# Two attention-and-mixer layers on one core: repacked score banks, an earlier buffer release, fillers in any dead bank, and an instruction order searched from a plan

## The chip, the cores and the metric

The kernel runs on one core of one Trainium2 chip. The metric is the device time of one execution in microseconds (us).

Five engines share the work: PE (TensorE, matmuls; its weight loads are listed as PEld), ACT (ScalarE), DVE (VectorE), POOL (GpSimd) and SP (SyncE, which issues DMA). A profile is one execution. "L955" is line 955 of that kernel, so the same instruction has another line number in each kernel.

## The reference

Two identical layers, each a layer norm, 16-head attention with a residual add, a layer norm and a mixer block with an MLP. S = 2048 tokens, D = 448, head size 28, F = 1792, bf16 inputs.

```python
def _A_ref(x, wqkv, wo):                 # attention, H = 16, Dh = 28
    q, k, v = ...                        # x @ wqkv, split into heads
    p = softmax(einsum("bhqd,bhkd->bhqk", q, k) * Dh ** -0.5)
    return merge_heads(einsum("bhqk,bhkd->bhqd", p, v)) @ wo

def _B_ref(x, w1, w2, w3, w4):           # mixer and MLP
    h = gelu(layernorm(x) @ w1)
    hs = concat(h's four quarters, shifted by +1, -1, +2, -2 tokens) @ w2
    x1 = x + hs
    return x1 + gelu(layernorm(x1) @ w3) @ w4

x = A_x                                  # the next two lines, twice
x = x + _A_ref(layernorm(x), A_wqkv, A_wo)
x = x + _B_ref(layernorm(x), B_w1, B_w2, B_w3, B_w4)
```

(The names are shortened here; the softmax is over the keys and the GELU is the tanh form.)

## The kernel before

A Python scheduler in the kernel's own file emits it. Every piece of work is a generator, a *task* with a priority. The scheduler has a model of how long each instruction takes and when its inputs are ready. It plays the kernel through in that model and so fixes one static order of instructions for each engine; the chip then runs these orders, with semaphores where engines depend on one another. What the model calls the end of the kernel is its *estimate*.

The 2048 tokens are 16 tiles of 128. A *unit* is a group of query tiles whose attention runs together: four units of four tiles in layer 0; in layer 1 three of four tiles (units 0 to 2) and two *half units* of two tiles (units 3 and 4). Scores go to five PSUM banks of 512 columns, in groups of three banks and two in turn; each group is one exponential on ACT. During attention a sixth bank takes the sums of P times V, and banks 6 and 7 serve everything else.

Score matmuls, with the two shapes. A half unit has only 256 queries, so it fills the 512 columns of a bank with two heads: one 64-row matmul over two heads' keys, against queries in which the other head's rows have been made zero.

```python
# q_proj, for a half unit: two copies of the queries, each with the other head's rows masked
if nw == 256:
    for h in (1, 0):
        yield op("dve", c_b2b(nw), lambda e, h=h: e.tensor_scalar(
            out=qT[:, g, q0 + 256*h : q0 + 256*h + 256], in0=qT[:, g, q0:q0 + 256],
            scalar1=cols[:, 2 + h:3 + h], scalar2=None, op0=ALU.mult), ...)
...
# st_ops: the scores of one group
for k, (si, i, j) in enumerate(grans[n]):
    ...
    bk = gbank(n) + k
    kc = kcol(L, kts[i])
    r0, rn = (32 * j, 32) if nt == 4 else (64 * j, 64)
    yield op("pe", ..., lambda e, ...: e.matmul(
        out=ps[:, bk, :], lhsT=kT[r0:r0 + rn, g, kc:kc + 128],
        rhs=qT[r0:r0 + rn, g, q0:q0 + 512], start=True, stop=True, tile_position=(r0, 0)), ...)
```

The mixer keeps its activations hT of eight tiles (HR = 8) in a ring. `t_mixA` (layer norm and w1) of a tile waits until the tile whose slot it takes, and that tile's neighbours, are finished. "Finished" means here: the whole MLP is done.

```python
def t_mixA(L, tiles, direct):
    for t in tiles:
        for tp in (t - HR - 1, t - HR, t - HR + 1):
            if 0 <= tp < NT:
                yield ("wait", ("mixBt", L, tp))
    ...                                    # statistics, normalise, transpose, w1, GELU into hT

def t_x1(L, t, i, xs):                     # spawned by t_mixB
    ...                                    # four w2 matmuls: the last readers of hT
    ...                                    # residual add, statistics, normalise

def t_mixB(L, tiles, direct, prio):
    ...                                    # t_x1 of each tile, w3, GELU, then per tile w4 and the residual add
        yield ("sig", ("x2", L, t))
        yield ("sig", ("mixBt", L, t))     # frees the slot in hT
```

Where its model sees PE idle, the scheduler puts in *fillers*, matmuls whose result nobody reads, put there to keep PE's clock up. They may use two of the eight banks:

```python
SC.fill = (0.13, lambda e, b: e.matmul(out=ps[:, bi(b), 0:256], lhsT=ident[:, :], rhs=wv[:, 0, 0:256], ...),
           ["b6", "b7"], ...)
...
for t in self.tasks: ...                   # a candidate of each task that is ready
    ...                                    # on PE and DVE a task of lower priority is held back where
                                           # it would delay one of higher priority
    key = (ready if eng == "act" else start, t[0], t[1])       # t[0] is the fixed priority
```

Some PSUM evacuations can go to DVE or ACT (`alt=[alt("act", ...)]`); the scheduler takes the engine that would end sooner. The softmax exponentials are always on ACT, and w3's results are copied by DVE and then given to ACT in one GELU over all 14 blocks (128x7168 for four tiles); only in the last unit does ACT take each block straight from PSUM.

## Time and profile before

| | before |
|---|---|
| median (lowest to highest) of 4 runs | 1169.1 us (1163.9 to 1169.3) |
| span of the profiled run | 1167.1 us |
| ACT busy, ACT idle | 1047.7, 119.4 us |
| last exponential ends; rest to the end ("tail") | 1080.9; 86.2 us |
| scheduler's own estimate | 1164.6 us |

The prediction below shows the lines of the page and of the timeline. Two further lines help to read it. The first is from the page of the kernel before: the chain that ended last, followed back from the end, as shares of the span.

```profile
ACT 44%; PE 39%; DVE 14%; DMA 1%; issue 1%; POOL 0%; SPq 0%; DVEq 0%
```

ACT is the busiest engine on the way to the end, but 39% and 14% are PE and DVE: the stretches where ACT waits. The second view gives busy time by stretch for the kernel before. Its columns are the stretch, its length, the busy time of PE, PEld, DVE, ACT and POOL with instruction counts, PE's granted clock (1.00 is full), the DMA share and GB/s. The stretches are the layer boundary, the middle of layer 1 and the tail.

```profile
525.20:556.00 30.80, 26.38 (x156) 13.06 (x155) 15.21 (x36) 14.52 (x9) 1.02 (x1) 0.97 0.14 33
787.80:875.30 87.50, 81.56 (x498) 26.63 (x498) 53.55 (x135) 71.94 (x65) 4.03 (x5) 0.80 0.09 23
1080.90:1167.10 86.20, 78.82 (x623) 50.55 (x617) 50.33 (x130) 27.90 (x61) 5.99 (x11) 1.00 0.11 30
```

Length minus ACT's busy time is ACT's idle time, which the prediction adds up; these three stretches hold 90 of the 119 us. From 796 to 808 PE is busy for 3.14, 2.70 and 2.86 of each 4 us, and the clock is 1.00; from 808 to 812 it is 0.73 and from 812 to 824 0.50.

### The profile page before, as it was taken

Reading aid. Unit: us, or ns where it says so; the run is one execution under the profiler, and the core shown is the slowest. Engines: PE = TensorE matmul, PEld = TensorE weight load, DVE = VectorE, ACT = ScalarE, POOL = GpSimd, SP = SyncE. Lnnn points to the kernel's source line nnn. Section 1 sums busy time; section 2 is a strip of 40 time slices with the busy share of each in tenths; the row PEclk is TensorE's granted clock in tenths of the full one; section 3 lists DMA queues with packets and bytes.
Section 4 is the critical chain, followed back from the end, with each engine's and each line's share of the span. In section 5 each row is a group of like instructions: output and inputs, shape, how many; then the busy total and the mean of one; then the engine's idle time right before and its main releaser. Section 6 shows DMA issues by size and latency. Waiting matters only on the chain.

```text
span 1167.1 us, 18576 instructions
## 1 busy us (share of the span) xinstructions
PE 1091.1 (93%) x7799; PEld 406.0 (35%) x7799; DVE 649.7 (56%) x1566; ACT 1047.7 (90%) x955; POOL 58.4 (5%) x76
## 2 busy tenths in 40 slices
PE   4899999989999999998999999998999999899998
PEld 1222333333332323334233323332333333333565
DVE  7876356523573255734767462557542574447952
ACT  5799999999999999994999999998889999999144
POOL 4000000000010000000001000000000010001000
PEclk9999999999999999999999999998779999999999
DMA  7122160000000000000111112321000110010011
GB/s 170 37 82 64 32 157 19 15 1 19 19 18 2 19 19 19 12 8 19 28 37 42 28 46 63 83 55 45 10 15 1 31 28 1 1 31 14 23 31 35
DMA packets 79213, 40.18 MB, mean 34 GB/s; under 512 B 63960, under 2 KB 72536, under 8 KB 79128
## 3 DMA queue, kind: packets, MB, share of 16 engines
q1 hardware_dynamic: 77544, 36.23, 12.2%
q0 software_dynamic: 1584, 2.75, 0.8%
q8 instruction: 61, 1.00, 0.3%
q14 instruction: 24, 0.20, 0.1%
HBM read 13.75 MB, written 8.13 MB: 19 GB/s over the span
## 4 chain that ended last, share of the span: by engine, by line
ACT 44%; PE 39%; DVE 14%; DMA 1%; issue 1%; POOL 0%; SPq 0%; DVEq 0%
ACT PT L955 38%; PE ps L932 9%; PE ps L979 7%; PE ps L1259 5%; PE ps L1239 4%; PE ps L1302 4%; ACT h2T L1254 4%; PE ps L695 3%; PE ps L756 2%; PE ps L1118 2%; DVE x1b L1194 1%; PE ps L715 1%; PE ps L1050 1%; DVE x_res L1197 1%; DVE st L1199 1%
## 5 line engine op out<-in xcount | busy, mean ns | idle before, releaser
L955 ACT ACTIVATE PT<-ps 128x1536 bf16<-128x1536 f32 (+1 forms) x821 | 940.2, 1258 | 45.9 <-PE ps L932 37.7
L932 PE MATMUL ps<-qT,kT 32*128 32x512 bf16 (+1 forms) x2048 | 335.8, 392 | 13.8 <-ACT PT L955 9.1
L979 PE MATMUL ps<-PT,vaug 128*32 128x512 bf16 (+1 forms) x2304 | 232.5, 368 | 3.1 <-ACT PT L955 1.8
L1302 PE MATMUL ps<-wv,ident 128*128 128x256 bf16 x1102 | 168.2, 279 | 8.8 <-DVE kT L704 2.2
L932 PEld LDWEIGHTS ps<-qT,kT 32*128 32x128 bf16 (+1 forms) x2048 | 79.4, 91 | 253.7 <-ACT PT L955 176.2
L1248 DVE CAST h2T<-ps 128x512 bf16<-128x512 f32 (+2 forms) x126 | 73.9, 586 | 113.0 <-PE ps L1239 112.2
L1239 PE MATMUL ps<-xT,w 128*128 128x512 bf16 (+3 forms) x672 | 129.0, 311 | 0.3
L1302 PEld LDWEIGHTS ps<-wv,ident 128*128 128x128 bf16 x1102 | 93.5, 99 | 82.3 <-issue 45.7
L1259 PE MATMUL ps<-w,h2T 128*128 128x448 bf16 x448 | 101.0, 358 | 11.4 <-ACT h2T L1254 11.4
L979 PEld LDWEIGHTS ps<-PT,vaug 128*32 128x32 bf16 x2304 | 57.2, 94 | 125.8 <-issue 88.6
L1262 DVE TENSOR_TENSOR x_res<-x_res,ps 128x448 f32<-128x448 f32 x32 | 19.8, 618 | 120.5 <-PE ps L1259 120.5
L1239 PEld LDWEIGHTS ps<-xT,w 128*128 128x128 bf16 x672 | 49.6, 97 | 58.4 <-issue 32.3
L1254 ACT ACTIVATE h2T<-h2T 128x7168 bf16<-128x7168 bf16 (+2 forms) x9 | 45.1, 5015 | 20.2 <-DVE h2T L1248 20.1
L1259 PEld LDWEIGHTS ps<-w,h2T 128*128 128x128 bf16 x448 | 38.7, 98 | 60.1 <-issue 19.5
L994 DVE COPY u_sb<-ps 128x512 f32<-128x512 f32 (+1 forms) x36 | 22.7, 629 | 37.1 <-PE ps L979 36.1
L1118 PE MATMUL ps<-xT,w 128*112 128x512 bf16 (+2 forms) x160 | 40.8, 364 | 0.6 <-DVE x1b L1194 0.6
L695 PE MATMUL ps<-xT,wk_pad 128*128 128x512 bf16 x128 | 39.8, 398 | 1.1 <-DVE qT L739 0.8
L695 PE MATMUL ps<-xT,wq_pad 128*128 128x512 bf16 (+1 forms) x144 | 38.6, 369 | 0.8 <-DVE qT L739 0.7
L1067 DVE TENSOR_SCALAR hT<-ps 112x512 f16<-112x512 f32 (+1 forms) x32 | 21.0, 655 | 31.0 <-PE ps L1118 31.0
L998 DVE SCALAR_TENSOR_TENSOR u_sb<-uin,fct,ps 128x512 f32<-128x512 f32 x24 | 17.9, 747 | 36.1 <-PE ps L979 34.2
L1050 PE MATMUL ps<-wo_pad,otn 128*128 128x448 bf16 x128 | 35.8, 362 | 2.0 <-DVE x_res L1054 1.3
L620 DVE BATCH_NORM_STATS2 st<-x_res 128x6 f32<-128x448 f32 x60 | 37.0, 618 | 1.0
(138 smaller groups left out, 852.0 us busy)
## 6 DMA issues: line engine op xcount, KB each, us to landing
uscr<-u_sb SPq DMA_DIRECT2D x24, 256.0 KB, 2.7
uin<-uscr SPq DMA_DIRECT2D x24, 256.0 KB, 2.8
x_res<-in_A_x_dram POOLq DMA_DIRECT2D x3, 896.0 KB, 12.0
out_dram<-uin SPq DMA_DIRECT2D x16, 112.0 KB, 1.7
w<-in_B_w_dram SPq DMA_DIRECT2D x1, 1568.0 KB, 15.6
w<-in_B_w_dram SPq DMA_DIRECT2D x1, 1344.0 KB, 10.7
h2T<-in_A_wqkv_dram SPq DMA_DIRECT2D x2, 336.0 KB, 6.5
xT<-xn SPq DMA_TRANSPOSE x37, 3.6
```

The source lines that it names most:

```text
L620: yield op("dve", 0.55, lambda e: e.bn_stats(out=st6[:, t, :], in_=w4[:, t, :] if staged else x_res[:, t, :]), reads=[("w4",) if staged el ...
L695: yield op("pe", c_mm(nw), lambda e, fc=fc, rows=rows, b=b: e.matmul(out=ps[:, bi(b), 0:nw], lhsT=wpad[0:rows, fc, 128 * g:128 * g + 128], ...
L932: yield op("pe", 0.225 if k == 0 else 0.005 if nt == 4 or k == 1 else 0.215, lambda e, bk=bk, r0=r0, rn=rn, g=g, kc=kc, q0=q0: e.matmul(ou ...
L955: yield op("act", 0.077 + 0.427 * cnt, lambda e, b0=b0, p0=p0, cnt=cnt: e.activation(out=PT[:, p0:p0 + cnt, :], in_=ps[:, b0:b0 + cnt, :], ...
L979: yield op("pe", 0.055 if nt == 4 else 0.035, lambda e, j=j, rhs=rhs, vs=vs, i=i: e.matmul(out=ps[32 * j:32 * j + 32, UBK, 0:128 * nt], lh ...
L1050: yield op("pe", c_mm(D), lambda e, g=g, tt=tt, b=b: e.matmul(out=ps[:, bi(b), 0:D], lhsT=otn[:, g, 128 * tt:128 * tt + 128], rhs=wo_pad[: ...
L1118: yield op("pe", c_mm(NW), lambda e, fc=fc, rows=rows, grp=grp, b=b: e.matmul(out=ps[0:112, bi(b), 0:NW], lhsT=w1[0:rows, fc, 112 * grp:11 ...
L1239: yield op("pe", c_mm(NW), lambda e, fc=fc, rows=rows, fch=fch, b=b: e.matmul(out=ps[:, bi(b), 0:NW], lhsT=w3[0:rows, fc, 128 * fch:128 * ...
L1248: yield op("dve", c_ps(NW), lambda e, fch=fch, b=b: e.tensor_copy(out=h2T[:, fch, hoff:hoff + NW], in_=ps[:, bi(b), 0:NW]), reads=[("ps", ...
L1254: yield op("act", c_act(14 * NW), lambda e: e.activation(out=h2T[:, :, hoff:hoff + NW], in_=h2T[:, :, hoff:hoff + NW], func=ACT.Gelu_apprx ...
L1259: yield op("pe", c_mm(D), lambda e, fch=fch, i=i, b=b: e.matmul(out=ps[:, bi(b), 0:D], lhsT=h2T[:, fch, hoff + 128 * i:hoff + 128 * i + 12 ...
L1302: SC.fill = (0.13, lambda e, b: e.matmul(out=ps[:, bi(b), 0:256], lhsT=ident[:, :], rhs=wv[:, 0, 0:256], start=True, stop=True), ["b6", "b ...
```

## The change

The intent, read from the diff, is fourfold: make the half units' score matmuls as cheap as the full units'; free a slot of hT as soon as nothing reads it any more; allow a filler in any bank whose contents are dead; and replace the fixed priorities by an order that comes from a plan, improved by a search.

```diff
@@ score banks of the half units: two key tiles of one head, no masked queries @@
-            if nw == 256:
-                for h in (1, 0):
-                    yield op("dve", c_b2b(nw), lambda e, h=h: e.tensor_scalar(...))
...
-                    r0, rn = (32 * j, 32) if nt == 4 else (64 * j, 64)
-                    yield op("pe", ..., lambda e, ...: e.matmul(
-                        out=ps[:, bk, :], lhsT=kT[r0:r0 + rn, g, kc:kc + 128],
-                        rhs=qT[r0:r0 + rn, g, q0:q0 + 512], start=True, stop=True, tile_position=(r0, 0)),
+                for (h, k, si, i, j) in sorted(mms):
+                    W = 128 * nt
+                    kt = kts[4 // nt * i + h]
+                    kc = kcol(L, kt)
+                    yield op("pe", ..., lambda e, ..., c0=W * h: e.matmul(
+                        out=ps[:, bk, c0:c0 + W], lhsT=kT[r0:r0 + 32, g, kc:kc + 128],
+                        rhs=qT[r0:r0 + 32, g, q0:q0 + W], start=True, stop=True, tile_position=(r0, 0)),
@@ early release of hT @@
-                        yield ("wait", ("mixBt", L, tp))
+                        yield ("wait", ("x1", L, tp))
...                                        # in t_x1, right after the four w2 matmuls
+            yield ("sig", ("x1", L, t))
@@ fillers @@
-                if self.busy.get(b, False):
+                if key(b) in self.live:
...
-                   ["b6", "b7"], ...
+                       ["b6", "b7", "b5", "b4", "b3", "b2", "b1", "b0"], ...
@@ order @@
-                for t in sorted(self.tasks, key=lambda x: (x[0], x[1])):
+                    todo.sort(key=self.rank)          # rank: the latest start in the plan
...
-            for grp in range(4):
+            def group(grp):                            # groups of a step become tasks of their own
...
+            yield from par(3, [group(grp) for grp in range(4)])
...
+        plan = None
+        for k in range(ROUNDS):                        # ROUNDS = 2
+            res = attempt(plan)
+            plan = res[2].latest_starts(res[0])
+        for seed in SEEDS:                             # 181 numbers
+            plan = reorder(plan, seed)
+        est, P, SC = attempt(plan)
```

`latest_starts` goes backwards through one played schedule and gives each instruction the latest time at which it may start without lengthening that schedule. `reorder` adds seeded random shifts to some of these times. Cut from the diff: memoisation in the scheduler, the bookkeeping of live banks, more places where loops become `par`, and new constants of the model (for instance PELAT from 0.12 to 0.04 and a table switch from 1.35 to 1.42).

## The prediction

> **What bounds the kernel now.** I read the page first: busy shares, then the forty slices, then the costliest groups.
>
> ```profile
> PE 1091.1 (93%) x7799; PEld 406.0 (35%) x7799; DVE 649.7 (56%) x1566; ACT 1047.7 (90%) x955; POOL 58.4 (5%) x76
> ...
> ACT  5799999999999999994999999998889999999144
> ...
> PEclk9999999999999999999999999998779999999999
> ...
> L955 ACT ACTIVATE PT<-ps 128x1536 bf16<-128x1536 f32 (+1 forms) x821 | 940.2, 1258 | 45.9 <-PE ps L932 37.7
> ```
>
> PE looks busiest, but its matmuls overlap and 168 us of its 1091 are the 1102 filler matmuls (L1302), there only to keep its clock up. The softmax exponentials on ACT, 821 of them, are 940 us of a 1167 us span, and slice after slice of ACT reads 9. So ACT is the bound, and **what can be won is ACT's idle time**, 1167.1 - 1047.7 = 119.4 us. The busy time by stretch says where it lies (stretch length minus ACT busy): start 0 to 27.9: 13.9; 27.9 to 58.4: 7.3; 58.4 to 525.2: 5.3; the layer boundary 525.2 to 556: 16.3; 556 to 787.8: 1.6; 787.8 to 875.3: 15.6; 875.3 to 1080.9: 1.1; the tail after the last exponential, 1080.9 to 1167.1: 58.3. Together 119.4.
>
> The timeline names three of these holes:
>
> ```profile
> 531.69 6.18 ACT L1254 ACTIVATE h2T<-h2T 128x7168 bf16<-128x7168 bf16 x1
> ...
> 556.01 2.37 ACT L955 ACTIVATE PT<-ps 128x1024 bf16<-128x1024 f32 x2 [16.24 <-PE ps L932]
> ...
> 803.04 7.80 ACT L955 ACTIVATE PT<-ps 128x1024 bf16<-128x1024 f32 x7 [4.41 <-PE ps L979]
> ```
>
> At the boundary, layer 1's scores need the first layer's MLP, whose GELU comes only at 531.7, when the attention of layer 0 is already over. In layer 1 a late normalisation stops ACT 4.4 us at 803, PE idles with it, and its clock drops (busy times in 4 us windows; the column after the engines is the granted clock):
>
> ```profile
> 812.00:816.00 4.00, 4.00 (x23) 1.06 (x16) 2.36 (x6) 3.53 (x4) 0.00 (x0) 0.50 0.24 53
> 816.00:820.00 4.00, 4.00 (x20) 1.03 (x19) 0.94 (x4) 2.96 (x3) 0.00 (x0) 0.50 0.29 66
> 820.00:824.00 4.00, 4.00 (x19) 0.78 (x16) 2.44 (x5) 2.47 (x3) 0.00 (x0) 0.50 0.01 2
> ```
>
> PE now really is full, and ACT runs 2.5 to 3.5 of 4 us. The same comes back at 856 to 868.
>
> The tail is a backlog of MLP work. A whole four-tile MLP, that of unit 2, runs after all attention is over, and only then does the last unit's chain begin (its statistics start at 1117.5):
>
> ```profile
> 1094.80 12.26 PE L1239 MATMUL ps<-xT,w 128*128 128x512 bf16 x56
> ...
> 1107.89 6.18 ACT L1254 ACTIVATE h2T<-h2T 128x7168 bf16<-128x7168 bf16 x1 [15.56 <-DVE h2T L1248]
> ...
> 1114.12 10.77 PE L1259 MATMUL ps<-w,h2T 128*128 128x448 bf16 x56 [1.22 <-ACT h2T L1254]
> ```
>
> Why so late? Unit 2's out-projection is done at 981.3, but its mixer's statistics wait until 1031.3:
>
> ```profile
> 1030.79 0.62 DVE L1262 TENSOR_TENSOR x_res<-x_res,ps 128x448 f32<-128x448 f32 x1 [5.61 <-PE ps L1259]
> 1031.33 0.62 DVE L620 BATCH_NORM_STATS2 st<-x_res 128x6 f32<-128x448 f32 x1
> ```
>
> They start 0.54 us after the second residual add of unit 1's MLP. That is the code's wait for "mixBt", the end of the whole MLP of the tile whose slot in the eight-tile ring hT is to be reused: 50 us of waiting.
>
> [...]
>
> **The change, part by part.**
>
> *Score banks of the half units* (last two units of layer 1). Before, a 64-row matmul of 512 columns made two heads against a zero-padded query, so only two row groups could run together and a three-bank group took two passes:
>
> ```profile
> 1001.41 0.60 PE L932 MATMUL ps<-qT,kT 64*128 64x512 bf16 x3
> ...
> 1002.48 0.39 PE L932 MATMUL ps<-qT,kT 64*128 64x512 bf16 x2
> ```
>
> After, two 32-row matmuls of 256 columns fill each bank and up to four heads run together. Matmuls become 2048 - 256 + 512 = 2304; a three-bank group should take 0.39, as the full units' x3 groups do. The number of banks is unchanged (32 items per segment either way), so ACT's 821 exponentials stay. 256 banks are some 51 pairs of groups: 51 x 0.21 = **10.7 us of PE time freed**, all of it between 945 and 1081, where PE has no slack. The 16 masking copies (L746, 283 ns) take 4.5 us off DVE, beside other work. On ACT directly: nothing.
>
> *The early release of hT* (signal after the w2 matmuls instead of after w4). Unit 1's w2 matmuls finish near 950 and unit 2's out-projection at 981, so the mixer of unit 2 can start some 50 us sooner. Its w3 and w4 (12.3 + 10.8 = 23 us of PE) then have to fit before 1081. Room: the 10.7 us freed, and the fillers of 787.8 to 1080.9, 183 at about 0.12 us each = 22 us (0.12 from runs such as 17 in 2.02 us). It fits, if the order is good. The tail then is the last unit's own chain: 9.5 us from the last exponential to its last out-projection add (1080.9 to 1090.4), plus 49.6 us from its statistics to the end (1117.5 to 1167.1) = 59; less about 5 because unit 3's two-tile w4 (1138.8 to 1144.2) can move into the chain's waits: 54. Against 86.2 that is -32. But the GELU of 6.18 us and two table loads, 8.7 us, move into attention, where ACT is full: **net -23**.
>
> *Order from an iterated plan.* Fixed priorities give way to latest start times of a previous plan, groups within one step become independent tasks, and 181 seeded shuffles were evidently kept because they shortened the modelled schedule. At the boundary, layer 0's last MLP is now recognised as critical; I take 12 of the 16.3 us as won, since a chain of projection, key maximum and bias (549 to 556, 7 us) is partly exposed. In 787.8 to 875.3 I take 12 of 15.6. At the start, 4 of the 7.3 us.
>
> *Filler in any dead bank.* It adds PE work only where the plan sees PE idle, and helps keep the clock at 1.00 when banks 6 and 7 are taken. Its gain is in the 12 just counted.
>
> Sum: -23 - 12 - 12 - 4 = -51, so 1169 - 51 = **1118 us**.
>
> **Rivals.** (1) *The freed PE time changes nothing*, because ACT is the bound: then only the order counts, the four-tile MLP stays in the tail, and the time is about 1169 - 28 = 1141. For it: ACT is 99% busy from 875 to 1081. Against it: the tail is PE work waiting for PE work, and 50 us of one wait is removed by the code. (2) *The plan is fitted to its own model*: static per-engine orders from 181 shuffles leave every wait tight, and small slips on the chip (more mode switches, fillers waiting for ACT, PE overrunning in 945 to 1081) open many small ACT waits. Before, waits of ACT on scores outside the named holes are only a few us; 20 us of such waits would give 1138. (3) *PE becomes the bound in the second half*, with half-clock spells as at 812: those cost about 11 us before; if they recur twice over, 1140. (4) *Better than counted*: all holes close and the tail shrinks to 48; the floor is 27.9 start + 1005.8 ACT work in attention + 8.7 moved + 48 = 1090.
>
> **Range and chances.** The terms are largely independent and each could fail by half, so I centre on 1118, with 1097 (most of rival 4) and 1141 (rival 1 or 2) as the ends of the 8 in 10 range. Two per cent is 23.4 us, below 1145.7: it takes two of the four terms failing to miss it. Faster 0.91, same 0.08, slower 0.01.
>
> **What would show it.** L955 still at 821 and near 940 us; score matmuls 2304 with 32 rows only, three-bank groups of the half units near 0.39 us; unit 2's mixer statistics before 1000 and its 128x7168 GELU before the last exponential; the tail 50 to 60 us; the hole at the boundary under 6 us; PEclk at 9 in all slices after the middle; ACT idle near 70 us in all. Wrong would be: a four-tile w3 still after the last exponential, ACT waits on scores spread over the whole of attention, or half-clock windows with more filler.

Figures for what it says of the chip, from the profile of the kernel before:

- *PE's matmuls overlap.* The 1792 score matmuls of 32 rows take 393 ns each in the mean, 704 us if added up, but PE is busy with them for 285.0 us.
- *Heads that run together.* Of the three 64-row matmuls at 1001.41 the first two start 3 ns apart and the third 0.22 us later. Of the 32-row matmuls of the full units three start within 7 ns at 700.26, and four within 10 ns at 27.24 and 555.36.
- *Mode switches.* After a filler matmul the next matmul starts 0.11 us later if it has a tile of the same shape (median of 890), 0.21 us later if it has 32 rows (median of 159).
- *Table loads.* Each of the 15 in attention and GELU takes 1283 ns. The GELU at 1013.96 starts 1.29 us after the start of its load, at 1012.67, and no idle time stands before the load.
- *No slack from 945 to 1081.* PE is busy for 127.3 of these 136 us, at a clock of 1.00.

## More of the kernel before

The runs were made on several chips, and every round ran the kernel before as well: its medians lay between 1168.3 and 1169.1 us.

## The result

| | before | after |
|---|---|---|
| median | 1169.1 us of 4 runs | 1130.3 us of 4 runs |
| lowest to highest | 1163.9 to 1169.3 | 1128.5 to 1136.5 |
| ratio, 95% interval | | 0.9688, 0.9641 to 0.9735 |
| ACT busy, ACT idle | 1047.7, 119.4 | 1056.2, 70.6 |
| tail after the last exponential | 86.2 | 49.6 |
| scheduler's own estimate | 1164.6 | 1125.7 |

A ratio is the mean time of one kernel's runs over the mean of the other's runs of the same rounds, so it is not quite the ratio of the medians beside it. The change is **faster by 3.1%**. The prediction was 1118 us within 1097 to 1141. The profiled run of the kernel after, used in all that follows, has a span of 1126.8 us.

From the page of the kernel after: busy times, the chain by engine, ACT and PE's clock in forty slices, and the exponentials.

```profile
PE 1063.9 (94%) x8094; PEld 407.6 (36%) x8094; DVE 613.8 (54%) x1527; ACT 1056.2 (94%) x972; POOL 55.7 (5%) x76
...
ACT  5899999999999999999789999999899999999954
...
PEclk9999999999999999999989999999899999999999
...
ACT 65%; PE 29%; DVE 3%; DMA 1%; issue 1%; SPq 0%; POOL 0%; ACTq 0%; DVEq 0%
...
L1108 ACT ACTIVATE PT<-ps 128x1536 bf16<-128x1536 f32 (+1 forms) x821 | 937.9, 1254 | 23.1 <-PE ps L1082 18.3
```

The exponentials are as many and as long as before (821; 940.2 and 937.9 us). What went down is the wait in front of them, 45.9 to 23.1 us, and the idle slices at the end: they read 1, 4 and 4 before and now 5 and 4. ACT carries 65% of the chain instead of 44%. But ACT's busy time *rose* by 8.5 us, which nobody had counted on.

The busy time of the kernel after by stretch, with the same three stretches (the boundary's is longer, because its holes now come later):

```profile
525.20:585.00 59.80, 56.92 (x350) 18.69 (x348) 43.70 (x109) 47.80 (x45) 3.04 (x3) 0.94 0.13 32
787.80:875.30 87.50, 81.86 (x577) 29.25 (x576) 61.26 (x154) 82.95 (x73) 6.51 (x7) 0.94 0.11 27
1077.20:1126.80 49.60, 43.65 (x400) 29.05 (x395) 27.39 (x72) 20.28 (x57) 3.73 (x7) 0.99 0.12 33
```

ACT's idle time there is 12.0, 4.6 and 29.3 us. Taking every stretch in this way gives the whole account, here against the prediction's terms:

| stretch (us of the span) | ACT idle before | after | moved | predicted |
|---|---|---|---|---|
| 0 to 58.4 | 21.2 | 17.4 | -3.8 | -4 |
| 58.4 to 525.2 | 5.3 | 0.9 | -4.4 | 0 |
| 525.2 to 787.8, the boundary and behind it | 17.9 | 13.8 | -4.1 | -12 |
| 787.8 to 875.3 | 15.6 | 4.6 | -11.0 | -12 |
| 875.3 to the last exponential | 1.1 | 4.7 | +3.6 | 0 |
| after the last exponential | 58.3 | 29.3 | -29.0 | -23 net |
| **ACT idle** | **119.4** | **70.6** | **-48.8** | **-51** |
| **ACT busy** | 1047.7 | 1056.2 | +8.5 | 0 |
| **span** | 1167.1 | 1126.8 | -40.3 | -51 |

Read the tail's row with care: the prediction's -23 is the tail's whole shortening (-32) less 8.7 us of ACT work that moves into attention. Measured in the same way, the tail is 36.6 us shorter, less 7.6 us of ACT work that left it.

The ACT timeline of the kernel after (start, length, what, in brackets the idle time before it and its releaser) shows the boundary and the tail:

```profile
514.07 6.18 ACT L1411 ACTIVATE h2T<-h2T 128x7168 bf16<-128x7168 bf16 x1
...
537.48 3.77 ACT L1108 ACTIVATE PT<-ps 128x1024 bf16<-128x1024 f32 x4 [3.17 <-PE ps L1082]
...
546.39 15.93 ACT L1108 ACTIVATE PT<-ps 128x1024 bf16<-128x1024 f32 x14 [5.13 <-PE ps L1082]
...
1061.51 6.18 ACT L1411 ACTIVATE h2T<-h2T 128x7168 bf16<-128x7168 bf16 x1
...
1069.00 8.23 ACT L1108 ACTIVATE PT<-ps 128x1536 bf16<-128x1536 f32 x7
```

The MLP's GELU at the boundary comes 17.6 us sooner (531.69 before), and the one hole of 16.24 us has become holes of 3.17 and 5.13 us and another of 3.14 at 580. The last four-tile GELU (1107.89 before) is at 1061.51, with seven exponentials still to come: that MLP's w3 and GELU have left the tail, and the rest of its w4 runs on beside the last unit's chain.

Two more views of the kernel after answer the prediction's lines. First DVE's timeline around the mixer of unit 2, then PE's timeline of one group of a half unit.

```profile
972.20 0.62 DVE L1207 TENSOR_TENSOR x_res<-x_res,ps 128x448 f32<-128x448 f32 x1
973.74 0.60 DVE L765 BATCH_NORM_STATS2 st<-x_res 128x6 f32<-128x448 f32 x1
```

```profile
1043.80 0.39 PE L1082 MATMUL ps<-qT,kT 32*128 32x256 bf16 x6
```

The mixer's statistics of unit 2 follow its own out-projection (L1207), no longer the MLP of another unit. A three-bank group of a half unit is six matmuls in 0.39 us, against 0.60 before.

Every sign that the prediction named for the tail is there. That does not yet show that the parts which it named are the *cause*: the change does four things at once.

### The profile page after: what moved, and what is told of

Its sections match the earlier page's. It is cut to its first block, busy times and chain, and to the rows that moved or that the text cites.

```text
span 1126.8 us, 19125 instructions
## 1 busy us (share of the span) xinstructions
PE 1063.9 (94%) x8094; PEld 407.6 (36%) x8094; DVE 613.8 (54%) x1527; ACT 1056.2 (94%) x972; POOL 55.7 (5%) x76
## 4 chain that ended last, share of the span: by engine, by line
ACT 65%; PE 29%; DVE 3%; DMA 1%; issue 1%; SPq 0%; POOL 0%; ACTq 0%; DVEq 0%
ACT PT L1108 58%; PE ps L1082 7%; PE ps L1132 5%; PE ps L1416 4%; PE ps L1395 4%; ACT h2T L1411 4%; PE ps L840 3%; PE ps L1464 2%; PE ps L897 1%; PE ps L1272 1%; DMA wv<-in_A_wqkv_dram 1%; ACT L1411 1%; ACT gt L1230 1%; PE ps L1203 1%; ACT L1108 1%; PE ps L860 1%
## 5 line engine op out<-in xcount | busy, mean ns | idle before, releaser
L1108 ACT ACTIVATE PT<-ps 128x1536 bf16<-128x1536 f32 (+1 forms) x821 | 937.9, 1254 | 23.1 <-PE ps L1082 18.3
L1082 PE MATMUL ps<-qT,kT 32*128 32x512 bf16 (+1 forms) x2304 | 322.7, 364 | 19.2 <-ACT PT L1108 13.5
L1132 PE MATMUL ps<-PT,vaug 128*32 128x512 bf16 (+1 forms) x2304 | 224.2, 366 | 2.8 <-ACT PT L1108 1.9
L1464 PE MATMUL ps<-wv,ident 128*128 128x256 bf16 x1141 | 174.3, 279 | 3.4 <-DMA wv<-in_A_wqkv_dram 2.4
L1082 PEld LDWEIGHTS ps<-qT,kT 32*128 32x128 bf16 x2304 | 80.9, 91 | 256.9 <-ACT PT L1108 141.2
L1395 PE MATMUL ps<-xT,w 128*128 128x512 bf16 (+3 forms) x672 | 123.5, 310 | 0.5 <-DVE h2T L1404 0.2
L1151 DVE SCALAR_TENSOR_TENSOR u_sb<-uin,fct,ps 128x512 f32<-128x512 f32 x24 | 17.9, 747 | 54.7 <-PE ps L1132 50.8
L1272 PE MATMUL ps<-xT,w 128*112 128x512 bf16 (+2 forms) x160 | 37.9, 362 | 2.5 <-DMA xT<-xn 2.0
L840 PE MATMUL ps<-xT,wk_pad 128*128 128x512 bf16 x128 | 35.8, 382 | 2.1 <-ACT kT L852 0.6
L1255 POOL TENSOR_TENSOR mst<-mst,neghalf 128x4 f32<-128x4 f32 (+2 forms) x10 | 9.3, 935 | 559.6 <-DVE mst L1254 559.1
L1359 POOL TENSOR_TENSOR mst<-mst,neghalf 128x1 f32<-128x1 f32 x32 | 19.3, 604 | 301.5 <-DVE mst L1357 301.1
## 6 DMA issues: line engine op xcount, KB each, us to landing
x_res<-in_A_x_dram POOLq DMA_DIRECT2D x3, 896.0 KB, 10.7
```

Of the source, the lines that this page charges most:

```text
L840: yield op("pe", c_mm(nw), lambda e, fc=fc, rows=rows, b=b: e.matmul(out=ps[:, bi(b), 0:nw], lhsT=wpad[0:rows, fc, 128 * g:128 * g + 128], ...
L1082: yield op("pe", 0.005 if ph == h else 0.012 + W / 2400.0, lambda e, bk=bk, r0=32 * j, g=g, kc=kc, q0=q0, W=W, c0=W * h: e.matmul(out=ps[: ...
L1108: yield op("act", e_dur(n), lambda e, b0=b0, p0=p0, cnt=cnt: e.activation(out=PT[:, p0:p0 + cnt, :], in_=ps[:, b0:b0 + cnt, :], func=ACT.E ...
L1132: yield op("pe", 0.004 + nt * 0.0133, lambda e, j=j, rhs=rhs, vs=vs, i=i: e.matmul(out=ps[32 * j:32 * j + 32, UBK, 0:128 * nt], lhsT=vaug[ ...
L1272: yield op("pe", c_mm(NW), lambda e, fc=fc, rows=rows, grp=grp, b=b: e.matmul(out=ps[0:112, bi(b), 0:NW], lhsT=w1[0:rows, fc, 112 * grp:11 ...
L1395: yield op("pe", c_mm(NW), lambda e, fc=fc, rows=rows, fch=fch, b=b: e.matmul(out=ps[:, bi(b), 0:NW], lhsT=w3[0:rows, fc, 128 * fch:128 * ...
```

## The experiments

**The theory** (the prediction's): the early release and the cheaper score matmuls take the MLP out of the tail, some 23 us net; the searched order closes the holes elsewhere, some 28 us. **Its rivals**: the order does most of it and would also do it with the old banks and the late release; the fillers' new banks carry a part through the clock; and the evacuations that went to ACT at the start cost part of the gain. All runs gave correct results. One caution holds for all of them: the scheduler plays the whole kernel anew after every edit, so each run has not only its edit but also another order of instructions.

### One part at a time, with the old priorities

**Release alone.** Kernel before, with the signal moved:

```diff
@@ t_x1, right after the w2 matmuls @@
+            yield ("sig", ("mixBt", L, t))
@@ t_mixB, after w4 @@
-                yield ("sig", ("mixBt", L, t))
```

> The kernel before with one line moved: the signal that frees a tile's slot of hT is given after the w2 matmuls instead of after w4. Theory A (my prediction): the 50 us wait of unit 2's mixer is gone and part of the four-tile MLP moves into attention, but PE has no spare time in 945 to 1081 while the half units' scores still take two passes, so about half of the tail's gain: 1150 to 1158. Rival (order alone matters): the old priorities put the freed work last again, 1165 to 1171. The planner's own model says 1151.0 (1164.6 for before).

Measured: 1157.2 us, ratio 0.9913 (0.9883 to 0.9944), so -0.87%. DVE's timeline and ACT's, in that order:

```profile
973.09 0.62 DVE L1054 TENSOR_TENSOR x_res<-x_res,ps 128x448 f32<-128x448 f32 x1
973.75 0.63 DVE L620 BATCH_NORM_STATS2 st<-x_res 128x6 f32<-128x448 f32 x1
```

```profile
1086.49 1.28 ACT L1255 ACT_TABLE_LOAD   x1
1096.37 6.18 ACT L1255 ACTIVATE h2T<-h2T 128x7168 bf16<-128x7168 bf16 x1 [8.60 <-DVE h2T L1249]
```

The wait of 50 us is gone, as the prediction read it from the code: the statistics start at 973.75 instead of 1031.33. And yet only some 11 us come of it. The table load for the GELU marks the end of attention, at 1086.49, and the GELU still waits 8.6 us for w3's results. The mixer got an earlier *start*, but under the old priorities PE found time for only about half of its 56 w3 matmuls before attention was over (they run from 1065 to 1094).

**Packing alone.** Kernel before, with the new score banks and without the masking copies:

```diff
-            if nw == 256:                              # masking copies, gone
-                    r0, rn = (32 * j, 32) if nt == 4 else (64 * j, 64)
+                for (h, k, si, i, j) in sorted(mms):   # two 32-row matmuls of 256 columns per bank
```

> The kernel before with the new score banks of the half units alone (32-row matmuls of 256 columns, two key tiles of one head a bank; no masking copies). Three-bank groups should fall from 0.60 to about 0.39 us, some 10.7 us of PE time. Theory A: PE time alone moves nothing while unit 2's mixer still waits for the end of unit 1's MLP, except that this MLP itself ends sooner: 1160 to 1169. Rival (PE time in the half units is the limit): the 10.7 us come off the end, 1158. The planner's own model says 1167.7.

Measured: 1171.2 us (20 runs), ratio 1.0019 (1.0003 to 1.0036): no gain, if anything a loss of 0.2%. PE's timeline shows that the packing itself works:

```profile
1043.10 0.40 PE L936 MATMUL ps<-qT,kT 32*128 32x256 bf16 x6 [0.23 <-ACT PT L962]
```

The groups take 0.40 us, so the 10.7 us of PE time are freed, but the end does not come sooner: PE waits for ACT at this group, and unit 2's mixer still waits for its slot in hT (its statistics start at 1024.34, right behind an add of the MLP before).

**Both**, with the old priorities:

```diff
+ the edits of the two runs above, together
```

> Both of the two changes, still with the old fixed priorities and fillers in banks 6 and 7. Theory A: they need each other, the four-tile MLP of unit 2 fits into attention, tail near 60 us: 1142 to 1149, that is more than the sum of e1 and e2. Rival (order alone): 1160 or more. The planner's own model says 1139.9.

Measured: 1146.8 us, ratio 0.9837 (0.9793 to 0.9881). ACT's timeline at the end of attention:

```profile
1078.70 1.55 ACT L962 ACTIVATE PT<-ps 128x1536 bf16<-128x1536 f32 x1
...
1081.56 6.18 ACT L1262 ACTIVATE h2T<-h2T 128x7168 bf16<-128x7168 bf16 x1
```

Together they bring 1.63%, more than the sum of 0.87% and -0.19%. This is the one place where the runs bear out the prediction's argument: the early start needs PE time before 1081, and packing supplies it. The scheduler's estimates go the same way (1164.6 before; 1151.0, 1167.7 and 1139.9), so a part of e2's loss is an order that the model itself rates longer. The GELU comes directly behind the last exponential. It just missed attention, so the tail is 62 us and not 54. The structure, under the old order, is worth about 21 us.

### The order, with and without the search

**Kernel after, without the 181 shuffles** (the plan's two rounds stay):

```diff
-    SEEDS = [96034, 609437, ...]
+    SEEDS = []
```

> The kernel after with the list of 181 seeds emptied; the plan of two iterations, the new banks, the early release and the fillers stay. Theory A: latest start times give most of the order, so 1135 to 1142, the seeds being polish. Rival (the seeds are the gain): 1150 to 1158. The planner's own model says 1150.5 (1125.7 with the seeds), so if the chip follows the model the rival is right and the plan alone is no better than the old priorities of e3.

Measured: 1151.1 us, ratio 0.9864 (0.9831 to 0.9897). That is no better than the old priorities with the same structure (1146.8). So **with this structure the plan by itself gained nothing; the search over it did**: 1151.1 to 1130.3, about 21 us. "The plan" stands here for the whole new scheduler without its shuffles: finer tasks, fillers in any dead bank and new model constants come with it. ACT's timeline at the boundary shows one place:

```profile
552.58 3.28 ACT L1096 ACTIVATE PT<-ps 128x1024 bf16<-128x1024 f32 x3 [7.51 <-PE ps L1070]
558.48 0.60 ACT L1096 ACTIVATE PT<-ps 128x512 bf16<-128x512 f32 x1 [2.62 <-PE ps L1070]
567.01 3.28 ACT L1096 ACTIVATE PT<-ps 128x1024 bf16<-128x1024 f32 x3 [7.94 <-PE ps L1070]
```

The one hole of 16.2 us has turned into three of 7.5, 2.6 and 7.9, together 18.1. The latest start times did *not* see layer 0's last MLP as critical in a way that helps.

**Old structure with the new scheduler, no shuffles:**

```diff
+    SEEDS = []
+            if nw == 256: ...                         # masking copies and 64-row matmuls back
-            yield ("sig", ("x1", L, t))                # after w2
+                yield ("sig", ("x1", L, t))            # after w4
```

> The scheduler of after with two plan iterations and no seeds, but with the score banks and the late hT release of before. If the structural parts carry as much under the new scheduler as under the old one (21 us in e3), this is some 20 us above e4: 1170. If the new scheduler makes the structure matter less, 1155 to 1160. The planner's own model says 1163.7 (e4: 1150.5, before: 1164.6).

Measured: 1154.9 us, ratio 0.9893 (0.9862 to 0.9924). With the plan and no search, the new structure is worth only 1154.9 - 1151.1 = 4 us, against 21 us under the old priorities; the intervals of the two ratios overlap, so even these 4 us are not shown.

On the old structure the new scheduler did gain, 1168.6 to 1154.9, and not by an order that its model rates shorter: the estimates are 1164.6 and 1163.7. But the mean granted clock was 0.996 in the profiled run, against 0.980 in the profile of the kernel before, with 1362 fillers against 1102. In 787.8 to 875.3 it was 0.96 against 0.80, and ACT's idle time there was 2.8 us against 15.6, nearly the whole gain. The clock is thus the likely cause; no run tests it apart from the rest of the scheduler.

DVE's timeline shows the slot wait is still there:

```profile
1014.09 0.61 DVE L1402 TENSOR_TENSOR x_res<-x_res,ps 128x448 f32<-128x448 f32 x1
1014.96 0.61 DVE L756 BATCH_NORM_STATS2 st<-x_res 128x6 f32<-128x448 f32 x1
```

Unit 2's out-projection adds end at 986.9, the statistics follow the MLP's add (L1402) at 1014.96, some 28 us later; before it was 50. The order alone had already halved that wait.

**Old structure with a search of its own.** This is the run that decides between the theory and its first rival. I ran a search for the previous kernel's structure: play the schedule, keep a shuffle if the estimate falls, 1812 rounds of three trials. It kept 125 seeds.

```diff
@@ against the run before @@
-    SEEDS = []
+    SEEDS = [...]                                      # 125 numbers, found for this structure
```

> The kernel of e5 (score banks and late hT release of before, new scheduler, fillers in any bank) with 125 seeds of its own, found the same way as those of after: random shuffles kept when they shorten the planner's own model, from 1163.7 to 1124.3. Theory A (the structural parts are needed to get the four-tile MLP into attention): the chip does not give it, 1142 or more. Rival (order alone does it, once it is searched for): 1118 to 1132, level with after or better.

Measured: 1126.8 us (6 runs), ratio 0.9656 (0.9622 to 0.9691). **Neither the packing nor the early release is in this kernel, and it is as fast as the changed kernel** (0.9677, 0.9637 to 0.9717, in the same rounds). DVE's timeline, then ACT's:

```profile
978.61 0.62 DVE L1410 TENSOR_TENSOR x_res<-x_res,ps 128x448 f32<-128x448 f32 x1 [0.20 <-PE ps L1407]
979.15 0.62 DVE L764 BATCH_NORM_STATS2 st<-x_res 128x6 f32<-128x448 f32 x1
```

```profile
960.92 6.18 ACT L1402 ACTIVATE h2T<-h2T 128x7168 bf16<-128x7168 bf16 x1
...
1065.77 1.45 ACT L1100 ACTIVATE PT<-ps 128x1536 bf16<-128x1536 f32 x1 [2.77 <-PE ps L1124]
...
1068.53 6.18 ACT L1402 ACTIVATE h2T<-h2T 128x7168 bf16<-128x7168 bf16 x1
```

The wait for the whole MLP is still in the code: the statistics at 979.15 follow the add at 978.61. But the search pulled that MLP forward. Its GELU is at 960.9, not at 1014.0 as in the kernel before, so the wait lasts from 966 to 979, 13 us and not 50. Unit 2's own GELU starts at 1068.53, just after the last exponential. The tail is 59.6 us and not 49.6; it is made up for elsewhere, since the last exponential ends at 1067.2, against 1077.2 in the changed kernel.

**The changed kernel again**, in the same rounds, to make that comparison fair:

```diff
  (no edit)
```

> The changed kernel itself once more, on the same chip as e9 and e10, to compare them with it directly: 1127 to 1137, the scatter seen so far.

Measured: 1129.9 us (1125.8 to 1136.4, 6 runs), ratio 0.9677. The result repeats. Its scatter goes with the clock: in order of time the six runs had mean granted clocks of 0.991, 0.991, 0.989, 0.987, 0.982 and 0.980.

**The changed kernel with a longer search**, 84 more seeds behind the 181:

```diff
     SEEDS = [
         ...
+        ...                                            # 84 more numbers
     ]
```

> After with 84 further seeds found in the same way; the planner's model goes from 1125.7 to 1113.2. If the chip follows the model as it did from before to after (38.8 of 38.9 us), 1117 to 1120. If the search has begun to fit what the model gets wrong, 1124 to 1131.

Measured: 1119.7 us, ratio 0.9591 (0.956 to 0.9622), about 0.9% below the changed kernel. The estimate went from 1125.7 to 1113.2, so the chip gave about 10 of the 12.5 us promised. The search had not been exhausted.

**The new structure with a search as long as the old structure's**, from the start and without the 181 seeds. It kept 90 seeds out of the same number of trials.

```diff
-    SEEDS = [96034, 609437, ...]
+    SEEDS = [...]                                      # 90 numbers, found for this structure
```

> The counterpart of e9 at equal search: the structure of after (new score banks, early hT release) from the unseeded plan of e4, with a search of exactly as many trials as e9's had (1812 rounds of three shuffles, same random start); 90 seeds were kept, the planner's model says 1115.3 (e9: 1124.3). If the structure is worth nothing once the order is searched for, it lies at e9's 1127: 1124 to 1130. If the structure keeps some of its value, the chip follows the model with the usual 4 to 6 us on top: 1118 to 1122, some 6 us under e9.

Measured: 1116.4 us (1115.2 to 1116.9), ratio 0.955 (0.9534 to 0.9565). This is the fastest version of all. From its page:

```profile
PE 1059.9 (95%) x8090; PEld 404.7 (36%) x8090; DVE 615.2 (55%) x1531; ACT 1052.4 (94%) x968; POOL 57.9 (5%) x76
...
ACT  5799999999999999999899999999989999999944
```

ACT is idle 1115.2 - 1052.4 = 62.8 us, 10.4 less than with the old structure and a search (1126.8 - 1053.6 = 73.2); 3.9 of these lie in the tail. Between the start and the tail only two slices read 8. The table of the six versions sums up this part (medians in us, the scheduler's estimate in brackets):

| | fixed priorities | plan | plan and search, equal effort |
|---|---|---|---|
| old banks, late release | 1168.6 (1164.6) | 1154.9 (1163.7) | 1126.8 (1124.3) |
| new banks, early release | 1146.8 (1139.9) | 1151.1 (1150.5) | 1116.4 (1115.3) |
| the structure is worth | 21.8 | 3.8 | 10.4 |

The structure is worth 22, 4 (not shown) or 10 us, depending on the order that is laid over it. Two searches of equal length were compared, one for each structure. How far two searches of one structure scatter was not measured, so the 10 us carry an unknown error; the ratio of the two ratios is 0.955 / 0.9656 = 0.989.

### The fillers and the evacuations

**Changed kernel, fillers in the two old banks only:**

```diff
-                       ["b6", "b7", "b5", "b4", "b3", "b2", "b1", "b0"], ...
+                       ["b6", "b7"], ...
```

> After, with its fillers allowed only in banks 6 and 7 as before. Theory A counted the wider choice of banks as part of a better clock in the middle of layer 1: then half-clock windows return and it takes 1135 to 1142. Rival: two banks are enough, nothing changes, 1128 to 1135. The planner's model, which has no clock in it, says 1125.7, the same as with all banks, with 1123 fillers in place of 1141.

Measured: 1133.4 us (1127.2 to 1140.6), ratio 0.971 (0.9655 to 0.9765). Against the changed kernel's 0.9688 (0.9641 to 0.9735) no difference is shown; the intervals lie over one another. Fillers fell only from 1141 to 1123. So no gain of this part is shown, and one of up to several us is not ruled out. In the stretch of 787.8 to 875.3, for which the prediction claimed it, the profile with two banks has a clock of 0.86 and 9.2 us of ACT idle time; the two profiles of the changed kernel have 0.94 and 0.92, 4.6 and 5.5 us. But the profiled run was the slowest of its four, so this stays open.

**Changed kernel, no fillers at all:**

```diff
-                       ["b6", "b7", "b5", "b4", "b3", "b2", "b1", "b0"], ...
+                       [], ...
```

> After without any filler matmul. If the fillers earn their PE time by the clock, the granted clock falls well under 0.95 and the time rises above 1150, with ACT waiting on scores in half-clock windows. If the clock would hold without them, the time is the model's 1139.3 plus the usual 5: 1140 to 1146.

Measured: 1216.3 us, ratio 1.0418 (1.0386 to 1.0451), 86 us (7.6%) above the changed kernel. The mean granted clock is 0.828, against 0.988. Three windows of 4 us, in the columns used above:

```profile
136.00:140.00 4.00, 2.47 (x18) 0.52 (x15) 0.00 (x0) 3.88 (x4) 0.00 (x0) 0.77 0.00 0
140.00:144.00 4.00, 3.40 (x22) 0.83 (x22) 1.51 (x4) 4.00 (x5) 0.00 (x0) 0.50 0.02 3
...
152.00:156.00 4.00, 2.56 (x14) 0.48 (x13) 0.00 (x0) 3.66 (x4) 0.00 (x0) 0.50 0.00 0
```

PE is busy for 2.5 to 3.4 of 4 us, and the clock falls from 1.00 (132 to 136) to 0.50. ACT still runs nearly through here (3.7 to 4.0 of 4 us). Of the 138 waits of score matmuls for an exponential in the whole run, 76.1 us together, none is longer than 1.6 us. The harm shows elsewhere: the exponentials' own wait rises from 23.1 us to 81.8 us, 73.4 of them for scores, since PE at the lower clock no longer keeps ahead (its score matmuls keep it busy for 368.3 us, against 322.7). The scheduler's model has no clock: its estimate is 1139.3, and this is the one run where it is badly off (by 77 us). The estimate is 13.6 us above that of the changed kernel, so that much of the 86 us can be the changed order; the rest the model does not see.

**Changed kernel, early evacuations kept on DVE.** In the changed kernel ACT does more casts and squares at the start: 12.4 us of them against 3.2 before. Is that the loss of 9 us? The groups of the changed kernel that do it:

```profile
L852 ACT ACTIVATE kT<-ps,cols 128x512 bf16<-128x512 f32 x6 | 4.1, 687 | 3.8 <-PE ps L840 3.8
L905 ACT ACTIVATE vaug<-ps 128x448 bf16<-128x448 f32 x6 | 3.3, 543 | 1.8 <-PE ps L897 1.8
```

```diff
-                for a in kw0.get("alt", ()):
+                for a in (kw0.get("alt", ()) if self.main >= 800 else ()):
```

> After, with the evacuations of the start (keys, queries, values) kept on DVE until the attention is nearly over; ACT busy should go from 1056 back to about 1047. If the 9 us that ACT spends on them were simply lost, the time falls by up to 9, to 1121 to 1125. If they were put where ACT had nothing else to do, or if the seeds fit only the order they were found for, it rises: the planner's model says 1140.5, so 1140 to 1146.

Measured: 1143.4 us, ratio 0.9803 (0.9763 to 0.9843), 13 us *slower* than the changed kernel, though ACT's busy time fell to 1044.1 us. ACT's timeline at the start:

```profile
46.21 4.62 ACT L1108 ACTIVATE PT<-ps 128x1536 bf16<-128x1536 f32 x4 [28.77 <-PE ps L1082]
```

Its first exponential waits 28.8 us for scores and starts at 46.2; in the changed kernel it starts at 40.3. The casts on ACT are paid for by scores that come sooner. A caution: the 181 seeds were found for the schedule *with* these casts, so part of the 13 us can be the misfit of the seeds. The run rules out that the casts were a plain loss that one could take back; it does not measure their worth.

## Why the prediction was right, and where it was not

The time was inside the range (1130 for 1118 predicted), the direction was right, and ACT's idle time was very nearly met: 70.6 us for "near 70". That near hit is partly luck, since errors of both signs cancel: the tail came out 6 us better than predicted and the stretch of 58.4 to 525.2 4.4 us, the boundary 8 us worse and the stretch before the last exponential 3.6 us. The reasons stand less well.

- **The sum was 11 us too good because ACT's busy time was taken as fixed.** The working "1167.1 - 1047.7" treats idle time as all that can change. ACT's work rose by 8.5 us: 9.2 us of casts and squares that the new order sends to ACT at the start and two more table loads (2.6 us), less some 3 us of slightly shorter work elsewhere. Idle fell by 48.8 us, the span by 40.3. This is the term that was missing, and it explains most of the 12 us between 1118 and 1130.
- **"Net -23" in the tail was about right in size, and its cause holds only in part.** The tail went from 86.2 to 49.6 us, a little better than the 54 predicted, and the 8.7 us of GELU and table loads did move into attention. But the step "Unit 1's w2 matmuls finish near 950 and unit 2's out-projection at 981, so the mixer of unit 2 can start some 50 us sooner" holds the *order* of everything else fixed. The old structure with a search reached 1126.8 without either part, and there the work waited for came sooner: the order alone cut the tail from 86.2 to 59.6 us. With the same amount of search the new structure has 50.1 us, with the GELU inside attention (1049.40, against 1068.53 and outside with the old), so the mechanism is real but smaller than was counted. And release and packing, each alone and under the old priorities, brought 1157 and 1171.
- **"It fits, if the order is good" was the key sentence and was passed over.** Under the old priorities the earlier start brought 11 us, with packing 21, and even then the GELU just missed attention.
- **"At the boundary, layer 0's last MLP is now recognised as critical; I take 12 of the 16.3 us"** was wrong twice. The plan alone left 18.1 us of holes there. With the shuffles, 3.17, 5.13 and 3.14 us remain, so 4.1 us were won and the sign "under 6 us" failed. Of the 8 us missing here, 4.4 were won in 58.4 to 525.2, which nobody predicted.
- **787.8 to 875.3: -12 predicted, -11.0 measured.** The clock there went from 0.80 to 0.94 and ACT's idle time from 15.6 to 4.6 us. The size is right. That the fillers' new banks did it is not shown: with two banks only, the whole time is the same within the interval, and ACT's idle time in this stretch (9.2 us) is already well below 15.6.
- **The start: -4 predicted, -3.8 measured, but this is luck.** ACT's idle time fell while its work rose by 9 us, so the first exponential came later (40.3 for 27.9). As soon as one counts progress and not idle time, the start *lost* some 4 us: the point where 100 us' worth of exponentials were done moved from 136.6 to 140.5.
- **The packing's own terms were exact**: 2304 matmuls, 0.39 us for a three-bank group, 821 exponentials unchanged. Alone they were worth nothing, as the prediction's first rival says of PE time when ACT is the bound. With the release they were worth about 10 us (1157.2 to 1146.8).
- **Rival 2, an order fitted to its own model, was the wrong way round.** The estimate was 1125.7 and the chip gave 1130. Over the twelve experiments the chip stayed within 8 us of the estimate, except for the old structure with the plan (9 us below) and the kernel without fillers (77 us above). The search found what the model promised and the chip gave it, all but a few us.
- **Rival 3, half-clock spells**, did not grow (the clock stood at 0.50 for 47.8 us in all in the profile before and for 27.3 us in that after, the longest spells being 20.5 and 6.8 us). There are some left, most of them too short for the slices, such as this window of the kernel after:

```profile
984.00:988.00 4.00, 3.96 (x36) 1.58 (x34) 0.42 (x2) 3.82 (x4) 0.00 (x0) 0.50 0.43 97
```

PE is full (3.96 of 4 us) at a clock of 0.50. The sign "PEclk at 9 in all slices after the middle" was met except for two slices that read 8. The stretch from 875.3 to the last exponential, where this window lies, lost 3.6 us.

What stays open: how much of the changed kernel's gain belongs to its structure. In the search of equal effort it was 10 us; in the changed kernel, with its own 181 seeds, the old structure with my search is just as fast. No run repeats a search with other random numbers, so the scatter of searches is not known.

## What to carry to other kernels

In this kernel with its static order, a freedom in the structure (an early release, cheaper passes) was worth only what the order made of it, and a searched order without it matched the changed kernel: test a structure with the order searched for both versions at equal effort, and test parts alone *and* together. A model of the schedule that comes within 0.8% of the chip (but for the kernel without fillers) makes a search over orders the strongest single tool here (1154.9 to 1126.8 and 1151.1 to 1116.4), while the new scheduler without a search brought 14 us with the old structure and nothing with the new. When you predict from the idle time of the bounding engine, ask also what the change will give that engine to do.
